# First keys and their tail in one tile, tails of four heads stacked, small loads as rows, and another order of the opening transfers

## The chip, the cores and the metric

One core of a Trainium2 chip. The metric is the device time of one execution in microseconds, as a median of several runs; smaller is better.

## The reference

Eight batches, each of eight heads, 576 tokens and 64 columns per head. 32 pack rows per head attend to keys and values; the tokens' queries then attend to the packed rows; the result, 512 wide, goes through one of eight experts.

```python
p_packed = sm_attn(p, k, v)               # (8, 8, 32, 64): 32 rows per head
out = sm_attn(q, p_packed, p_packed)      # (8, 8, 576, 64)
x = out.transpose(0, 2, 1, 3).reshape(8, 576, 512)
logits = x @ w_gate                       # 8 experts
local_gate = sigmoid(x @ w_local)
...
e = argmax(logits[b, s]) if s == 0 or local_gate[b, s] < 0.5 else prev_e
p = softmax(logits[b, s])
out[b, s] = p[e] * (relu(x[b, s] @ w1[e]) @ w2[e])
```

The kernel computes every token of a batch with the expert of the batch's first token, and computes a batch again where a count of other tokens says so; with these inputs that count is nought.

## The kernel before, in words

All of a batch's attention is small beside the two layers of its expert. The first layer (`layer1`, L939) multiplies the attention weights by the product of packed values and w1, split in a high and a low part (wph, wpl; `pack_quarters`, L870 to L882 in the first batch); the second layer (`layer2`, L967 to L976) multiplies by w2, split likewise (`splits`, L925 and L927). Heads are handled in two sets Q of four.

For the first batch, nothing can be hidden behind another batch, and the expert must be known before its weights can be loaded. So the opening is a chain: packs and keys are loaded (`loads`, `load_packs`, `load_tokens`) and turned in place on VectorE (`turn_keys`, L377); scores of a Q are 32-row products on TensorE, with the 64 tail tokens of a head as products of their own (`scores`, L443 and L453); VectorE takes their minima (L463, L474), ScalarE the exponential (L488), TensorE turns the weights (`keys`, L497 and L501), multiplies by the values (L521) and turns the packed values (L541). `early_choice` computes the first token's expert from q0, its eight query columns (L682 to L714); `gate_weights` (L655) needs wgl, which holds w_gate and w_local. The expert's number goes to SyncE (`choose`, L672), which then issues the weights (`weights`, L823 and L836, in the order of `FIRST`). Meanwhile the queries of the first batch, and the keys and queries of the second, are turned by TensorE transposes and ScalarE copies, head by head (`turn_tokens`, L391, L392, L394), and `queries` (L571) and `soften` (L591 to L635) make the attention weights of the tokens, in two parts.

Each of these is a generator. A planner (`weave`) steps them in an order that it works out while the program is built: `Clock` holds a due time for each engine and tile, from prices in the code (`price`, L98 to L125; a DMA by its bytes over `clock.rate`, plus 2000 ns while it starts before 25 us, L137 to L153). The result is a fixed order of instructions per engine, and each engine runs its own in order. Where TensorE would be without work by that clock, `keep_warm` adds fillers, products of ones that nobody reads (L214, two passes each), one for each 240 ns of the gap (`FILL`, L1149), until the third piece of the first layer. Work of a batch later than the one that still lacks its expert is stepped only when the engines named in `by` are free in the planner's clock (the factor 0.0 in L1139); before, the second batch's turns need only their data.

DMAs are issued in order by SyncE (nc.sync) or ScalarE (nc.scalar), the issuing engine waiting for a free buffer first. Buffers are counted by tag in `BUFS`: five of "kv", two of "w1t", eight of "w2s", five of "o", two of "p_in". The first batch's keys and values take four of the five "kv" buffers and its queries start on the fifth.

## Time and profile before

| | us |
|---|---|
| median of 3 runs | 431.51 (431.38 to 431.62) |
| the profiled execution | 431.04 |
| its span | 429.0 |
| TensorE matmuls busy | 413.5 (96%) |
| VectorE busy | 295.4 (69%) |
| ScalarE busy | 178.8 (42%) |

The span runs from the first to the last instruction that the profile shows; some 2 us of the time lie around it. Busy time of TensorE counts fillers too, and the ends of matmuls are modelled, so 96% doesn't mean that it works at its peak. Where a line of the profile gives a count for TensorE, it counts passes: a product of 32-bit floats takes two, a transpose of 128 rows one. Times below are from the start of the span.

### The profile page before, as it was taken

Reading aid. Unit: us, or ns where it says so; the run is one execution under the profiler, and the core shown is the slowest. Engines: PE = TensorE matmul, PEld = TensorE weight load, DVE = VectorE, ACT = ScalarE, POOL = GpSimd, SP = SyncE. Lnnn points to the kernel's source line nnn. Section 1 sums busy time; section 2 is a strip of 40 time slices with the busy share of each in tenths; the row PEclk is TensorE's granted clock in tenths of the full one; section 3 lists DMA queues with packets and bytes.
Section 4 is the critical chain, followed back from the end, with each engine's and each line's share of the span. In section 5 each row is a group of like instructions: output and inputs, shape, how many; then the busy total and the mean of one; then the engine's idle time right before and its main releaser. Section 6 shows DMA issues by size and latency. Waiting matters only on the chain.

```text
span 429.0 us, 10275 instructions
## 1 busy us (share of the span) xinstructions
PE 413.5 (96%) x3958; PEld 329.0 (77%) x3959; DVE 295.4 (69%) x859; ACT 178.8 (42%) x419; POOL 36.3 (8%) x56
## 2 busy tenths in 40 slices
PE   8799999999999999998999999999999999999994
PEld 8666688867887688777887688777887688878883
DVE  4368679798974797838877697838877697546221
ACT  1356734265333544254443643345433544244221
POOL 2000620300110002000030002000020002000000
PEclk9999999999999999999999999999999999999999
DMA  8889799367998289976999199964999340634011
GB/s 226 183 257 317 229 135 154 84 243 229 141 162 295 73 220 131 152 273 200 168 146 317 63 242 136 187 242 149 197 122 273 113 147 0 235 122 147 0 63 56
DMA packets 167271, 73.24 MB, mean 171 GB/s; under 512 B 129072, under 2 KB 147248, under 8 KB 167216
## 3 DMA queue, kind: packets, MB, share of 16 engines
q1 hardware_dynamic: 166528, 72.13, 75.5%
q8 instruction: 33, 0.54, 0.6%
q10 hardware_dynamic: 688, 0.39, 0.3%
q14 instruction: 22, 0.18, 0.2%
HBM read 63.07 MB, written 9.44 MB: 169 GB/s over the span
## 4 chain that ended last, share of the span: by engine, by line
PE 73%; DMA 9%; DVE 8%; SPq 6%; issue 2%; ACT 1%; POOLq 0%; DVEq 0%; POOL 0%; ACTq 0%
PE bank L967 33%; PE bank L939 19%; DMA qn<-in_q_dram 6%; SPq L307 4%; PE bank L972 3%; PE bank L976 3%; DVE wpl L913 2%; PE bank L571 2%; PE bank L521 2%; PE bank L899 2%; PE bank L443 2%; DVE qn L555 1%; PE bank L497 1%; DMA kv<-in_q_dram 1%; PE bank L391 1%
## 5 line engine op out<-in xcount | busy, mean ns | idle before, releaser
L967 PE MATMUL bank<-w2s,h 128*128 128x512 f32 x768 | 207.3, 400 | 3.9 <-DVE w2s L927 3.2
L967 PEld LDWEIGHTS bank<-w2s,h 128*128 128x128 f32 x768 | 135.4, 188 | 35.6 <-DVE w2s L927 4.9
L954 DVE SCALAR_TENSOR_TENSOR h<-bank,h 128x256 fp32r<-128x256 f32 x192 | 61.3, 347 | 60.0 <-ACT h L950 59.4
L950 ACT ACTIVATE h<-bank 128x256 fp32r<-128x256 f32 (+1 forms) x128 | 52.7, 412 | 118.7 <-PE bank L939 111.1
L939 PEld LDWEIGHTS bank<-a2h,wph 128*128 128x128 f32 x256 | 47.0, 188 | 16.2 <-ACT wph L910 1.3
L939 PE MATMUL bank<-a2h,wpl 128*128 128x320 f32 (+1 forms) x256 | 56.3, 298 | 0.4 <-DVE wpl L913 0.2
L939 PE MATMUL bank<-a2h,wph 128*128 128x320 f32 (+1 forms) x256 | 56.4, 301 | 0.2
L939 PE MATMUL bank<-a2l,wph 128*128 128x320 f32 (+1 forms) x256 | 54.9, 296 | 0.0
L635 POOL TENSOR_TENSOR a2l<-a2t,a2h 128x576 fp32r<-128x576 f32 (+2 forms) x17 | 23.0, 1355 | 294.6 <-ACT a2h L632 294.6
L939 PEld LDWEIGHTS bank<-a2h,wpl 128*128 128x128 f32 x256 | 41.3, 188 | 1.8 <-DVE wpl L913 1.6
L939 PEld LDWEIGHTS bank<-a2l,wph 128*128 128x128 f32 x256 | 40.9, 188 | 0.0
L925 ACT CAST w2s<-w2raw 128x512 fp32r<-128x512 f32 x64 | 37.4, 622 | 2.8 <-DMA w2raw<-in_moe_w_dram 2.8
L927 DVE TENSOR_TENSOR w2s<-w2raw,w2s 128x512 fp32r<-128x512 f32 x58 | 37.4, 680 | 1.3 <-ACT w2s L925 1.3
L972 PE MATMUL bank<-w2s,h 128*128 128x512 f32 x64 | 25.3, 396 | 0.0
L976 PE MATMUL bank<-w2s,h 128*64 128x512 f32 x64 | 25.0, 391 | 0.0
L591 DVE STREAM_TRANSPOSE sT<-bank 128x288 f32<-128x288 f32 (+2 forms) x36 | 13.2, 420 | 10.4 <-ACT gate L589 8.4
L913 DVE TENSOR_TENSOR wpl<-bank,wph 128x512 fp32r<-128x512 f32 x28 | 18.0, 680 | 2.4 <-ACT wph L910 2.4
L910 ACT CAST wph<-bank 128x512 fp32r<-128x512 f32 x28 | 14.9, 595 | 10.8 <-PE bank L899 10.8
L488 ACT ACTIVATE a<-a,nb 128x576 f32<-128x576 f32 x16 | 12.4, 776 | 16.3 <-DVE nb L474 16.3
L463 DVE TENSOR_SCALAR_CACHE_REDUCE a<-bank 128x288 f32<-128x288 f32 (+2 forms) x36 | 13.6, 421 | 6.0 <-PE bank L453 3.8
L632 ACT CAST a2h<-a2t 128x576 fp32r<-128x576 f32 (+2 forms) x18 | 11.2, 622 | 13.8 <-DVE a2t L626 9.5
L214 PE MATMUL bank<-warm 128*128 128x128 f32 x88 | 15.8, 335 | 1.1 <-DVE warm L209 1.1
(139 smaller groups left out, 454.0 us busy)
## 6 DMA issues: line engine op xcount, KB each, us to landing
w2raw<-in_moe_w_dram SPq DMA_DIRECT2D x64, 256.0 KB, 6.3
w1t<-in_moe_w_dram SPq DMA_DIRECT2D x14, 1024.0 KB, 6.7
kv<-in_v_dram SPq DMA_DIRECT2D x16, 512.0 KB, 6.5
out_dram<-o SPq DMA_DIRECT2D x31, 256.0 KB, 2.3
qn<-in_k_dram SPq DMA_DIRECT2D x24, 288.0 KB, 7.1
qn<-in_q_dram SPq DMA_DIRECT2D x24, 288.0 KB, 6.9
kv<-in_q_dram SPq DMA_DIRECT2D x8, 256.0 KB, 4.5
w1t<-in_moe_w_dram SPq DMA_DIRECT2D x4, 512.0 KB, 7.3
```

The source lines that it names most:

```text
L214: nc.tensor.matmul(out=warm_ps[:, :128], lhsT=warm, rhs=warm, start=True, stop=True)
L307: nc.sync.dma_start(out=x[ps_].rearrange("i h (c j) -> i (h c) j", j=32), in_=rows[r, a])
L635: eng.tensor_tensor(out=a2l, in0=a2t, in1=a2h.bitcast(F32), op=ALU.subtract)
L913: nc.vector.tensor_tensor(out=lo[fh][:, Q], in0=ts[fh, Q], in1=hi[fh][:, Q].bitcast(F32), op=ALU.subtract)
L925: nc.scalar.copy(out=w[:, 0], in_=raw)
L927: (nc.gpsimd if st["early"] and c > 1 else nc.vector).tensor_tensor(out=w[:, 1], in0=raw, in1=w[:, 0].bitcast(F32), op=ALU.subtract)
L939: nc.tensor.matmul(out=t[:, :GROUP * (m1 - m0)], lhsT=st["wp"][c // 4][wi][:, Q, fs], rhs=a2[ai][Q][:, GROUP * m0:GROUP * m1], start=(n == ...
L950: nc.scalar.activation(out=h[:, :w], in_=t[:, :w], func=AF.Relu)
L954: nc.vector.scalar_tensor_tensor(out=h[:, dst:dst + z - a], in0=t[:, a:z], scalar=0.0, in1=h[:, a:z].bitcast(F32), op0=ALU.max, op1=ALU.su ...
L967: nc.tensor.matmul(out=acc, lhsT=hs[hi], rhs=w[:, wi], start=(c == 0 and n == 0), stop=(c == NC - 1 and n == 2),)
L972: nc.tensor.matmul(out=acc, lhsT=h[:, 256:WIDE + TAIL], rhs=w[:, 0], start=(c == 0), stop=False, skip_group_check=True,)
L976: nc.tensor.matmul(out=acc[0:TAIL], lhsT=h[:, 256:WIDE], rhs=w[:, 1], start=False, stop=(c == NC - 1), skip_group_check=True,)
```

## The change

- The first batch's keys and their tail lie in one tile "kf" on the tag "w1t" (later the first weights' buffers), 5 x 64 columns per head. Q0's keys come in two transfers of two heads on SyncE and its tail on ScalarE's queue; all four pack transfers are on ScalarE's queue. A turn of the packs is a step of its own, ahead of the keys'.
- A score product takes the tail's 32 columns along: 160 columns where r is 0 or 1, 128 else. The products of the tail (L453) are gone.
- The 64 tail tokens of four heads are loaded as one 128 x 128 tile (tag "w2s", before "o"), and turned by one transpose and one copy. The other 512 tokens come in one transfer with four tokens per partition; they are turned two heads at a time, four transposes and one copy of 512 columns.
- q0 and w_local are loaded as sixteen rows of 64 (tile "small") on ScalarE's queue, after Q0's keys, turned by TensorE and copied to their places by VectorE; w_gate follows on the same queue.
- The second batch's packs are loaded after its keys and queries, not ahead of them. The first batch's query turns wait for both Q's value products, the second batch's turns for both first parts of the first batch's `queries`.
- In `keys` of the first batch the tail's transpose shares the bank that ScalarE reads.

```diff
...
+    small = const.tile([2 * H, D], F32, name="small")
...
+    def load_keys(Q):
+
+        x = tile_([128, HQ, (NJ + 1) * D], F32, "kf", "w1t")
+        rows = k[0].rearrange("(h q) s d -> q h s d", q=NQ)[Q]
+        clock.rate = 300.0
+        for hs in (slice(0, HQ // 2), slice(HQ // 2, HQ)) if Q == 0 else (slice(0, HQ),):
+            nc.sync.dma_start(out=x[:, hs, 0:NJ * D], in_=rows[hs, 0:512].rearrange("h (p c) d -> p h (c d)", c=NJ))
+        clock.rate = 200.0
+        (nc.scalar if Q == 0 else nc.sync).dma_start(out=x[0:TAIL, :, NJ * D:], in_=rows[:, 512:S].rearrange("h p d -> p h d"))
+        return x
+
+    def load_small():
+
+        clock.rate = 100.0
+        nc.scalar.dma_start(out=small[0:H], in_=q[0, :, 0, :])
+        nc.scalar.dma_start(out=small[H:2 * H], in_=w_local.rearrange("(h d) e -> h (d e)", d=D))
+        with nc.allow_non_contiguous_dma(reason="rows of 8 elements"):
+            nc.scalar.dma_start(out=wgl[:, :, 0:E], in_=w_gate.rearrange("(h d) e -> d h e", d=D))
+
+    def turn_small():
+
+        yield need(small, banks=1, when=lambda: sts[0]["scored"] > 0)
+        tp = bank()
+        nc.tensor.transpose(out=tp[0:D, 0:2 * H], in_=small, identity=ident[0:2 * H, 0:2 * H])
+        yield need(tp, by=("DVE",))
+        nc.vector.tensor_copy(out=q0[:, :, 0:1], in_=tp[0:D, 0:H].unsqueeze(2))
+        nc.vector.tensor_copy(out=wgl[:, :, E:E + 1], in_=tp[0:D, H:2 * H].unsqueeze(2))
+        give(tp)
+        sts[0]["small"] = True
...
     def load_pairs(src, b, Q):
 
-        x = tile_([128, HQ, 2, 2 * D], F32, "kv")
-        rest = tile_([TAIL // 2, HQ, 2 * D], F32, "qt", "o")
+        x = tile_([128, HQ, NJ * D], F32, "kv")
+        rest = tile_([128, 2 * D], F32, "qt", "w2s")
         rows = at(src, b).rearrange("(h q) s d -> q h s d", q=NQ)[Q]
-        clock.rate = 320.0
-        for c in range(2):
-            nc.sync.dma_start(out=x[:, :, c], in_=rows[:, 256 * c:256 * c + 256].rearrange("h (p r) d -> p h (r d)", r=2))
+        clock.rate = 300.0
+        nc.sync.dma_start(out=x, in_=rows[:, 0:512].rearrange("h (p c) d -> p h (c d)", c=NJ))
         clock.rate = 200.0
-        nc.sync.dma_start(out=rest, in_=rows[:, 512:S].rearrange("h (p r) d -> p h (r d)", r=2))
+        nc.sync.dma_start(out=rest, in_=rows[:, 512:S].rearrange("h (p r) d -> h p (r d)", r=2))
         return x, rest
...
-            st["p"] = load_packs(b, (nc.sync, nc.scalar, nc.sync, nc.scalar))
+            st["p"] = load_packs(b, (nc.scalar,) * 4)
...
-            order = (("p", 1), ("k", 0), ("k", 1), ("q", 0), ("q", 1)) if st["second"] else \
+            order = (("k", 0), ("k", 1), ("q", 0), ("q", 1), ("p", 1)) if st["second"] else \
...
+            yield need(slot="p_in" if name == "p" else "qn" if blocks else "kv" if name == "v" else "w1t" if st["early"] and name == "k" else ("kv", "w2s"))
...
-                st[name, Q] = load_tokens(x, b, Q) if name == "k" and st["early"] else load_pairs(x, b, Q)
-            if st["early"] and (name, Q) == ("v", 1):
-                clock.rate = 100.0
-                with nc.allow_non_contiguous_dma(reason="512 elements"):
-                    nc.sync.dma_start(out=q0[:, :, 0:1], in_=q[0, :, 0:1, :].rearrange("h s d -> d h s"))
-                    nc.sync.dma_start(out=wgl[:, :, 0:E], in_=w_gate.rearrange("(h d) e -> d h e", d=D))
-                    nc.sync.dma_start(out=wgl[:, :, E:E + 1], in_=w_local.rearrange("(h d) e -> d h e", d=D))
+                st[name, Q] = load_keys(Q) if name == "k" and st["early"] else load_pairs(x, b, Q)
+            if st["early"] and (name, Q) == ("k", 0):
+                load_small()
...
-        yield need(slot="qn", when=lambda: (name, 0) in st and (st["second"] or "a2t" in st))
+        yield need(slot="qn", when=lambda: (name, 0) in st and ("a2t" in st if st["early"] else sts[0]["asked"] >= NQ))
...
-            yield need(when=lambda: (name, Q) in st)
+            yield need(when=lambda: (name, Q) in st and (st["second"] or st["valued"] == NQ and (Q == 0 or st["ppT"][Q] is not None)))
             x, rest = st[name, Q]
-            for h in range(HQ):
-                yield need(x, rest, banks=1, by=("Activation",))
+            for hs in (slice(0, 2), slice(2, 4)):
+                yield need(x, banks=1, by=("Activation",))
                 tp = bank()
-                for c in range(2):
-                    nc.tensor.transpose(out=tp[:, 128 * c:128 * c + 128], in_=x[:, h, c], identity=ident)
-                nc.tensor.transpose(out=tp[:, 256:HALF], in_=rest[:, h], identity=ident[:TAIL // 2, :TAIL // 2])
+                for n in range(4):
+                    nc.tensor.transpose(out=tp[:, 128 * n:128 * n + 128], in_=x[:, hs][:, n // 2, 128 * (n % 2):128 * (n % 2) + 128], identity=ident)
                 yield need(tp, by=("Activation",))
-                nc.scalar.copy(out=xT[:, Q, h], in_=tp[:, :HALF])
+                nc.scalar.copy(
+                    out=xT[:, Q, hs, 0:256].rearrange("a h (p c) -> a h c p", c=2), in_=tp.rearrange("a (h c p) -> a h c p", h=2, c=2),
+                )
                 give(tp)
+            yield need(rest, banks=1, by=("Activation",))
+            tp = bank()
+            nc.tensor.transpose(out=tp[:, 0:128], in_=rest, identity=ident)
+            yield need(tp, by=("Activation",))
+            nc.scalar.copy(out=xT[:, Q, :, 256:HALF], in_=tp[:, 0:128].rearrange("a (h x) -> a h x", h=HQ))
+            give(tp)
...
-            yield need(when=lambda: ("k", Q) in st and "p" in st)
-            yield need(*st["k", Q])
-            for x in st["k", Q]:
-                turn(x)
-
-            st["kT", Q] = st["k", Q][0].rearrange("a h (c x i) -> a h x c i", c=NJ, x=2)
-        if Q == 0:
+            yield need(when=lambda: ("k", Q) in st and "pT" in st)
+            x = st["k", Q]
+            yield need(x)
+            for y in (x[:, 0:2, 0:NJ * D], x[:, 2:4, 0:NJ * D]) if Q == 0 else (x[:, :, 0:NJ * D],):
+                nc.vector.transpose(out=y, in_=y)
+            y = x[0:TAIL, :, NJ * D:]
+            nc.vector.transpose(out=y, in_=y)
+
+            st["kT", Q] = x.rearrange("a h (c x i) -> a h x c i", c=NJ + 1, x=2)
...
+    def turn_packs(st):
+
+        yield need(when=lambda: "p" in st)
+        yield need(st["p"])
+        turn(st["p"])
+        st["pT"] = st["p"].rearrange("a h (x n) -> a h x n", n=NP)
...
+                    cs = NJ + (r < 2)
                     for h in range(HQ):
                         nc.tensor.matmul(
-                            out=ts[Q, r][32 * h:32 * h + 32, :512 // n if n == 4 else HALF],
+                            out=ts[Q, r][32 * h:32 * h + 32, :32 * cs if n == 4 else HALF],
                             lhsT=st["pT"][ps_, NQ * h + Q, x],
-                            rhs=st["kT", Q][ps_, h, x] if st["early"] else st["kT", Q][ps_, h],
-                            start=(x == 0), stop=(x == steps - 1),
-                        )
-            for x in range(steps if st["early"] else 0):
-                for r in range(2):
-                    ps_ = slice(rows * r, rows * r + rows)
-                    for h in range(HQ):
-                        nc.tensor.matmul(
-                            out=ts[Q, r][32 * h:32 * h + 32, 128:160],
-                            lhsT=st["pT"][ps_, NQ * h + Q, x],
-                            rhs=st["k", Q][1][ps_, h, NP * x:NP * x + NP],
+                            rhs=st["kT", Q][ps_, h, x, 0:cs] if st["early"] else st["kT", Q][ps_, h],
                             start=(x == 0), stop=(x == steps - 1),
                         )
...
-            nc.tensor.transpose(out=tps[1][:TAIL, 256:384], in_=sc[:, 512:S], identity=ident)
+            rest = tps[0 if st["early"] else 1][:TAIL, 256:384]
+            nc.tensor.transpose(out=rest, in_=sc[:, 512:S], identity=ident)
             if st["early"]:
...
-            nc.scalar.copy(out=a_rest[Q][:TAIL], in_=tps[1][:TAIL, 256:384])
+            nc.scalar.copy(out=a_rest[Q][:TAIL], in_=rest)
...
+        st["valued"] += len(Qs)
...
-        if part != 0:
-            st["asked"] += len(Qs)
-        if st["asked"] == NQ:
+        st["asked"] += len(Qs)
+        if st["asked"] == NQ * (1 + st["early"]):
...
+        yield need(when=lambda: None not in st["ppT"] and "small" in st)
+        yield need(*st["ppT"], wgl, banks=1)
...
+            yield need(when=lambda: st["ppT"][Q] is not None and "small" in st)
...
+                    *((turn_packs(st), early_choice(st), turn_small()) if early else ()),
...
```

## Rows read from the trace of the kernel before

**Rows 1.** Busy time by stretch, core 0: from:to in us, length, then TensorE (PE), weight loads (PEld), VectorE (DVE), ScalarE (ACT) and GpSimd (POOL) busy with their instructions, granted clock, DMA share, GB/s; and the line of the fillers from the groups of instructions from 0 to 45 us (busy us, mean ns | idle before).

```profile
0.00:38.20 38.20, 33.74 (x548) 26.47 (x549) 20.52 (x77) 14.53 (x41) 3.31 (x18) 1.00 0.86 236
...
45.00:424.00 379.00, 372.94 (x3349) 298.15 (x3335) 269.76 (x766) 159.44 (x367) 31.73 (x37) 1.00 0.76 163
...
L214 PE MATMUL bank<-warm 128*128 128x128 f32 x88 | 15.8, 335 | 1.1 <-DVE warm L209 1.1
```

**Rows 2.** The chain that ended last, from 26.9 to 45 us, in order of time: start us, us, what.

```profile
28.06 0.37 PE bank L391 x2
28.43 0.17 PE bank L392
...
33.37 0.59 PE bank L870 x16
33.96 1.09 PE bank L214 x8
...
36.78 0.38 PE bank L571 x16
...
38.25 1.08 PE bank L939 x6
...
42.48 0.64 PE bank L214 x4
```

**Rows 3.** Timeline of TensorE's matmuls from 0 to 45 us: start us, us, engine, line, operation, out<-in, passes [idle before, releaser].

```profile
1.10 8.09 PE L214 MATMUL bank<-warm 128*128 128x128 f32 x44 [1.10 <-DVE warm L209]
9.12 0.96 PE L443 MATMUL bank<-kv,p_in 32*32 32x128 f32 x57
...
9.98 0.47 PE L453 MATMUL bank<-kt,p_in 32*32 32x32 f32 x29
...
14.72 0.32 PE L453 MATMUL bank<-kt,p_in 32*32 32x32 f32 x22 [2.11 <-issue]
...
20.18 1.03 PE L521 MATMUL bank<-kv,a1T 128*32 128x64 f32 x32
...
26.12 0.31 PE L704 MATMUL bank<-gate,et 128*32 128x32 f32 x4
...
28.53 0.51 PE L571 MATMUL bank<-qn,ppT 64*32 64x160 f32 x16
```

**Rows 4.** The DMA view of short windows. First a queue's line in 11.50 to 11.75 us (packets, MB, share of 16 engines), then issues (out<-in, queue, operation, count, KB each, median us from issue to landing): packs of the first batch issued on ScalarE's queue in 1.2 to 1.7 us, the first keys' tail in 2.2 to 2.9, w_local in 9.2 to 10.3, packs of the second batch in 15.85 to 17.8, the first weights in 28.5 to 29.

```profile
q8 instruction: 1, 0.02, 40.5%
...
p_in<-in_p_dram ACTq DMA_DIRECT2D x2, 64.0 KB, 2.8
...
kt<-in_k_dram SPq DMA_DIRECT2D x1, 64.0 KB, 4.4
...
wgl<-in_moe_w_local_dram SPq DMA_DIRECT2D x1, 2.0 KB, 5.1
...
p_in<-in_p_dram SPq DMA_DIRECT2D x4, 32.0 KB, 5.2
...
w1t<-in_moe_w_dram SPq DMA_DIRECT2D x1, 512.0 KB, 3.8
```

**Rows 5.** Timeline of VectorE from 0 to 45 us, columns as in group 3.

```profile
8.00 0.66 DVE L377 STREAM_TRANSPOSE p_in<-p_in 128x512 f32<-128x512 f32 x1
8.59 1.20 DVE L377 STREAM_TRANSPOSE kv<-kv 128x1024 f32<-128x1024 f32 x1
9.72 0.39 DVE L377 STREAM_TRANSPOSE kt<-kt 64x256 f32<-64x256 f32 x1
...
11.49 0.16 DVE L474 TENSOR_REDUCE nb<-m 128x1 f32<-128x4 f32 x1
...
22.84 0.25 DVE L690 STREAM_TRANSPOSE es<-bank 128x64 f32<-128x64 f32 x1 [1.08 <-PE bank L682]
...
24.84 0.24 DVE L701 STREAM_TRANSPOSE et<-es 128x64 f32<-128x64 f32 x1
...
27.37 0.14 DVE L669 TENSOR_SCALAR e<-ecd 1x1 int32<-1x1 f32 x1
...
35.75 0.75 DVE L882 TENSOR_TENSOR wpl<-bank,wph 128x256 fp32r<-128x256 f32 x2
```

**Rows 6.** ScalarE: two lines of its timeline from 0 to 40 us (columns as in group 3), its line of copies from the groups of 0 to 45 us, and the page's group of 512-column casts (busy us, mean ns | idle before, releaser).

```profile
1.76 1.28 ACT L488 ACT_TABLE_LOAD   x1 [1.63 <-PEq L1256]
11.68 0.78 ACT L488 ACTIVATE a<-a,nb 128x576 f32<-128x576 f32 x1 [8.64 <-DVE nb L474]
...
L394 ACT COPY qn<-bank 128x288 f32<-128x288 f32 x24 | 9.4, 400 | 4.9 <-PE bank L392 4.1
...
L910 ACT CAST wph<-bank 128x512 fp32r<-128x512 f32 x28 | 14.9, 595 | 10.8 <-PE bank L899 10.8
```

**Rows 7.** Timeline of the DMAs that SyncE's queue issues, from 0 to 60 us: start us, us that the issue took, line, out<-in, count.

```profile
1.73 0.45 SPq L277 DMA_DIRECT2D kv<-in_k_dram  x1
...
7.75 1.46 SPq L368 DMA_DIRECT2D wgl<-in_moe_w_gate_dram  x1
...
10.47 3.22 SPq L289 DMA_DIRECT2D kv<-in_q_dram  x2
...
14.35 0.92 SPq L289 DMA_DIRECT2D kv<-in_q_dram  x2
...
28.54 0.40 SPq L836 DMA_DIRECT2D w1t<-in_moe_w_dram  x1
```

15 lines of the change are left out of this document (5 added, 10 removed).

## The prediction

> **What bounds the kernel now.** I read the busy times by stretch first [rows 1]. Between 45 and 424 us TensorE is busy 372.9 of 379 us, so nothing can be won there but by less TensorE work, and the change leaves that stretch alone. Up to the first product of the network's first layer, at 38.2 us, it is idle for 4.5 us, and a good part of its busy time is filler: 88 passes of L214, 15.8 us in all. The reader is to see that the time is the moment at which the first layer starts, plus the TensorE work still undone then, plus a tail that stays.
>
> Then the chain of waits [rows 2]: from 28 us on it holds TensorE alone, and in its order turns, fillers and packing of weights alternate until L939 at 38.25. There the length of TensorE's own queue sets the time, fillers included. Then TensorE's timeline ahead of that [rows 3]: 44 filler passes, scores of Q0 at 9.12, scores of Q1 broken off for 2.11 us by nothing that the profile names, the values' products of Q1 at 20.18, the early choice's product at 26.12. The DMA view shows what the break may be [rows 4]: the core's one instruction packet of that time starts between 11.5 and 11.75 us, when the queue is full of 4-byte elements (w_local's 2 KB take 5.1 us to land). Then VectorE [rows 5], ScalarE [rows 6] and SyncE's issues [rows 7]: the choice's last step ends at 27.51, the first weights are issued at 28.54.
>
> **The change part by part**, on the clock of the profiled run (span 429.0 us, its time 431.04, so 2.04 us outside; the median 431.51 is 0.47 above it). The planner decides the order and the number of fillers; I work its due times by hand from the code. They give order and counts, no times. Durations are the rows'.
>
> *First transfers.* Key and pack transfers start together: the first half of the keys is the first issue of SyncE, not the third at 1.73 [rows 7]; ScalarE issues four pack pieces at some 0.45 each by 2.6, the last landing at 2.6 + 2.8 = 5.4 at worst, the tail, fifth on that queue, by 3.4 + 4.4 = 7.8 [rows 4]. VectorE, done with packs and keys by 7 (0.66 and 1.20 [rows 5]), needs 0.39 for the tail. Ready about 7.5 to 8.3, against 8.66 before. It gains nothing: the planner waits for all of tile kf, whose last transfer, the tail, is due at 6524 ns; 160 later TensorE, at 5400 after the first 10 fillers, gets (6684 - 5400)/240 = 5; three turns make the scores due at 8626, and (8626 - 6542)/240 = 8 more: 23, where the same working for the kernel before gives 10 + 4 + 8 = 22, and 22 of two passes are the 44 of the row [rows 3]. Two more passes at 1.09/8 = 0.136 [rows 2]: the scores of Q0 start at 9.4, 0.25 later. That hides 1.1 to 1.9 us of late landing; without the cover such lateness would count in full.
>
> *Scores of 160 columns.* 64 passes for 96: 57 passes took 0.96 with 0.27 of latency in it, 12 ns each, and half are a quarter longer: 0.85 for 1.26 from 9.12 to 10.45. VectorE's minima and nb need 1.2 after (10.45 to 11.65): nb at 11.45. Exp 0.78 [rows 6], at 12.3. The planner has 9 fillers here (18 passes, 2.45 us), so L497 at 12.8.
>
> *Keys of Q1.* In the planner's order their turn now comes behind Q0's minima (it stood ahead at 8.59 [rows 5]): 1.20 + 0.39 from 11.45, scores of Q1 at 13.35 to 14.2, nb at 15.35. The break of 2.11 us: before, it came after 44 + 96 + 8 + 74 passes, with a weight load each; now as many are run through only some 24 passes into the values' products, at 14.4, and the packet that it may wait for is asked for no later. Cost between 0 and 2.1; I take 0, since the only such packet's long wait fell on 1,024 four-byte elements that are now sixteen rows.
>
> *Values, second Q.* Exp 15.4 to 16.2, L497 at 16.5, products at 17.8 (before 20.18), the packed values' transpose at 19.4, since a unit of query turns stands ahead of it. The a_rest copy without its wait on VectorE saves 0.2, included.
>
> *The choice.* Gate products by 20.5; VectorE's chain took 22.84 to 25.08, 2.24, to which I add 0.1 for a ScalarE copy ahead of its exp: 22.85. L704 comes 1.1 after that chain before; now no second batch's turn can stand there (it needs "asked" of both Q), only a query unit and one filler: 23.2. e0 ended 1.4 after L704's start (26.12 to 27.51), with transposes of VectorE in between; without them 1.0: 24.2, 3.3 earlier. SyncE: its last issues ahead (q of Q1 and four pack pieces, 0.45 each) wait for a kv buffer read at about 20.2 and end at 23.3, so they are no block. Weights issued at 25.25, landed at 29.05 [rows 4].
>
> *Turns of four heads.* Before, a head is 0.37 + 0.17 = 0.54, a unit of four 2.16 [rows 2]. After, nine 128-wide transposes of 0.185: 1.67. Six units: 2.9 us less TensorE work. ScalarE: 4 copies of 0.400 become two of about 0.6 (the 512-column copy's 0.595) and one of 0.26: 1.46 for 1.60 [rows 6]. So L571 of Q1 at 23.45 to 23.9 (before 28.53).
>
> *From there to the first layer.* VectorE's way from that L571 to the end of wpl took 28.53 to 36.5, 8.0; it would allow 31.4, and 1.5 more if VectorE has to wait for the second batch's packs, now loaded last (issued by 23.3, landing up to 5.2 later, 28.5 [rows 4], with its softmax queued behind): 31.4 to 32.9. TensorE's queue is longer: of the second batch's four units I count 2.1 in the planner's gap (22.7 to 30.3 on its clock, 7.6, less 2.0 for other ScalarE work, at 2.7 each), 3.5 us; L870 0.59, two L571 0.76, and 18 fillers of two passes (7.6 less 3.3 planned work, by 0.24), 4.9: 23.9 + 9.75 = 33.7 for 38.2, 4.5 earlier. Undone are 1.9 units, 3.2 us, where before three heads (1.62) and 0.64 of filler were: 0.9 given back. Net 3.6.
>
> *The other way round:* TensorE work less 2.9 + 0.8; idle 4.5 to 1.4, 3.1 less; fillers 118 passes for 88, 4.0 more: 2.8. I take the middle of 2.8 and 3.6, near 3.3: 428.2 on the median. Its own range 426.0 to 430.2: 1.1 less if no filler costs more than its cover, 2.1 more for the break.
>
> A page of the Trainium skill, "Runtime: NRT & Kernel Launch", section "Instruction fetch mechanics", speaks against the gain from the break: instruction blocks are fetched ahead and crossing one is mostly hidden. By that rule the 2.11 us would have another cause and stay; the trace, with one packet and one break side by side, speaks against it, but it shows that only once.
>
> **The rivals.** *More:* the units of the second batch fit before the first layer entirely, in place of fillers. 33.0 for L939 and nothing left: 38.2 - 33.0 + 1.62 + 0.64 = 7.4, so 424.1. For it: TensorE has 9 us there, the work is 6.7 + 1.4; against: the planner starts a unit of a later batch only when ScalarE is free in its own clock. *The break stays* wherever it now falls, on the chain since Q1's way sets all that follows: 3.3 - 2.1 = 1.2, so 430.3. For it: the data queue is as full as before. *Slower:* ScalarE, in order, is held by its own eight transfers. The same small loads on SyncE were followed by two query issues that took 3.22 instead of 0.92 [rows 7], because the queue took no more. If w_gate's issue holds ScalarE until w_local's landing before, 14.4, its table load of 1.28 [rows 6] and exp follow at 15.7 for 11.5: 4.2 less 3.3, 0.9 slower, 432.4. It decides from an exp later than 14.9; at 10 or less it costs nothing. Against: that queue now holds 0.34 MB, not 2.5. *The change does nothing:* should every unit of the second batch fall behind the first layer (6.7 us undone, 5.1 more, less 0.6 of filler), 4.5 is given back in full: 431.5.
>
> **How the numbers follow.** Chances: forecast 0.54, more 0.16, the break stays 0.13, nothing 0.08, slower 0.09. What a measurement can tell from no change is about 0.2%, 0.9 us: faster is under 430.65. The break case lies at that border and I give it 0.10 faster, 0.03 same. Faster 0.80, same 0.11, slower 0.09. The range 424.0 to 431.6 leaves out the slower case, and the half of the first rival below its value.
>
> **What would show it.** Right: 46 filler passes ahead of scores at 9.3 to 9.5; no break of more than 0.5 us before 20; first weights issued at 24.5 to 26; L939 at 33 to 34.5 with about two units of L391 after it; TensorE's busy time from 45 on unchanged in its steps. Wrong: exp of Q0 after 13; L939 later than 36; a wait of VectorE on p_in of over 1 us amid its softmax; new idle time of TensorE between L939 and 60 us on w2s or w1t.

## The result, and the profile after

The changed kernel takes 435.92 us (435.73 to 436.10), the kernel before on the same chip 431.56 (431.38 to 431.83): a ratio of 1.01, 95% interval 1.0083 to 1.0118, 4.4 us slower, where 428.2 was forecast with 424.0 to 431.6 as its range. Its profiled execution has a span of 434.0 us, the forecast's was 425.7 (428.2 less 2.04 around the span and the 0.47 between median and profiled run). In the changed file L443 is L486 (scores), L488 L521 (exp), L497 L530, L521 L555 (values' products), L704 L738, L836 L870 (issue of the first matrix's quarters, w1t), L870 L904 (their product), L939 L973 (first layer), L967 L1001 (second layer); a unit of turns is L416 twice and L424 once. Some executions of a kernel run at a lower granted clock throughout; the ratios leave them out, and the profiled one of e15 below is of that kind.

TensorE's timeline of the changed kernel from 0 to 50 us, in the columns of [rows 3]:

```profile
1.10 6.75 PE L214 MATMUL bank<-warm 128*128 128x128 f32 x46 [1.10 <-DVE warm L209]
13.32 1.63 PE L486 MATMUL bank<-kf,p_in 32*32 32x160 f32 x64 [5.47 <-DVE kf L449]
...
15.04 3.71 PE L214 MATMUL bank<-warm 128*128 128x128 f32 x20
...
29.08 0.31 PE L738 MATMUL bank<-gate,et 128*32 128x32 f32 x4
...
38.19 0.56 PE L973 MATMUL bank<-a2h,wph 128*128 128x320 f32 x2
...
40.86 2.40 PE L214 MATMUL bank<-warm 128*128 128x128 f32 x20
...
46.38 0.67 PE L904 MATMUL bank<-w1t,ppT 64*32 64x256 f32 x16 [0.84 <-DMA w1t<-in_moe_w_dram]
```

The 46 filler passes are there as predicted, but they end at 7.85, and TensorE then waits 5.47 us for the tail of the keys. The scores of Q0 start at 13.32 (9.12 before [rows 3], 9.4 forecast). All the same the first layer starts at 38.19, where it did before (38.18). The choice's product is at 29.08 (26.12 before, 23.2 forecast). So the whole loss against the kernel before stands behind that point: from it to the end are 395.8 us, before 390.8, and 392.0 in the forecast. The forecast is missed twice, by 4.5 us ahead of the first layer and by 3.8 behind it.

VectorE's timeline of the same run, its two waits for the first transfers:

```profile
10.44 0.71 DVE L402 STREAM_TRANSPOSE p_in<-p_in 128x512 f32<-128x512 f32 x1 [8.76 <-DMA p_in<-in_p_dram]
...
12.83 0.44 DVE L449 STREAM_TRANSPOSE kf<-kf 64x256 f32<-64x256 f32 x1 [0.49 <-DMA kf<-in_k_dram]
```

ScalarE's timeline, the transfers that it issues (ACTq: start, duration of the issue) and its first work:

```profile
0.78 4.39 ACTq L344 DMA_DIRECT2D p_in<-in_p_dram  x4
5.73 0.76 ACTq L280 DMA_DIRECT2D kf<-in_k_dram  x1
...
10.14 0.66 ACTq L289 DMA_DIRECT2D wgl<-in_moe_w_gate_dram  x1
10.82 1.28 ACT L521 ACT_TABLE_LOAD   x1 [10.70 <-DMA p_in<-in_p_dram]
16.13 0.78 ACT L521 ACTIVATE a<-a,nb 128x576 f32<-128x576 f32 x1 [4.02 <-DVE nb L507]
```

The four packs took 4.39 us to issue, not 1.8, and were there at 10.44; the tail, fifth on that queue, at 12.83. The DMA view of 4 to 8 us says whose packets were served (q1 is SyncE's queue, q10 ScalarE's: packets, MB, share of 16 engines; then issues of that stretch with us from issue to landing):

```profile
q1 hardware_dynamic: 1252, 1.04, 98.6%
q10 hardware_dynamic: 495, 0.12, 14.0%
...
p_in<-in_p_dram ACTq DMA_DIRECT2D x1, 64.0 KB, 5.6
kf<-in_k_dram ACTq DMA_DIRECT2D x1, 64.0 KB, 7.1
```

Both queues are fed, q10 gets 2 packets of some 250 bytes to 5 of some 830, a tenth of the bytes. Last, busy time by stretches of 1 us (columns as in [rows 1]; the third number from the end is TensorE's granted clock):

```profile
9.00:10.00 1.00, 0.00 (x0) 0.00 (x0) 0.00 (x0) 0.00 (x0) 0.00 (x0) 1.00 1.12 210
10.00:11.00 1.00, 0.00 (x0) 0.00 (x0) 0.56 (x1) 0.17 (x1) 0.00 (x0) 0.89 1.13 324
11.00:12.00 1.00, 0.00 (x0) 0.00 (x0) 1.00 (x3) 1.00 (x1) 0.00 (x0) 0.50 0.68 122
...
17.00:18.00 1.00, 1.00 (x8) 1.00 (x8) 0.69 (x4) 0.00 (x0) 0.00 (x0) 0.70 0.71 216
```

TensorE, idle from 7.85 on, was granted 0.50 (1.2 of 2.4 GHz) from 11 to 17 us; the 20 filler passes behind the first scores then took 3.71 us (18 in 2.45 were forecast), the scores themselves 1.63 (1.12 at the full clock, as in e4 below).

### The profile page after: what moved, and what is told of

Read it like the earlier page. It is cut to its first block, busy times and chain, and to the rows that moved or that the text cites. A ratio compares the mean times of both kernels' runs of the same rounds, so it can differ in the third digit from the quotient of the medians.

```text
span 434.0 us, 10237 instructions
## 1 busy us (share of the span) xinstructions
PE 414.8 (96%) x3939; PEld 332.5 (77%) x3940; DVE 295.0 (68%) x862; ACT 178.0 (41%) x413; POOL 36.6 (8%) x56
## 4 chain that ended last, share of the span: by engine, by line
PE 77%; DVE 8%; DMA 8%; issue 2%; ACT 2%; SPq 1%; POOLq 0%; POOL 0%; DVEq 0%; ACTq 0%
PE bank L1001 35%; PE bank L973 20%; PE bank L1006 3%; PE bank L1010 3%; DMA qn<-in_q_dram 3%; DMA kf<-in_k_dram 3%; PE bank L486 2%; PE bank L555 2%; DVE wpl L947 2%; PE bank L214 2%; PE bank L933 2%; DMA w1t<-in_moe_w_dram 2%; PE bank L606 2%; PE bank L530 2%; DVE qn L590 1%
## 5 line engine op out<-in xcount | busy, mean ns | idle before, releaser
L1001 PE MATMUL bank<-w2s,h 128*128 128x512 f32 x768 | 207.9, 400 | 4.5 <-DVE w2s L961 3.1
L1001 PEld LDWEIGHTS bank<-w2s,h 128*128 128x128 f32 x768 | 135.3, 188 | 36.1 <-issue 5.3
L973 PEld LDWEIGHTS bank<-a2h,wph 128*128 128x128 f32 x256 | 47.1, 188 | 16.7 <-issue 1.7
L973 PE MATMUL bank<-a2h,wph 128*128 128x320 f32 (+1 forms) x256 | 56.8, 302 | 0.1
L973 PE MATMUL bank<-a2h,wpl 128*128 128x320 f32 (+1 forms) x256 | 56.3, 298 | 0.4 <-DVE wpl L947 0.2
L973 PE MATMUL bank<-a2l,wph 128*128 128x320 f32 (+1 forms) x256 | 54.6, 294 | 0.0
L973 PEld LDWEIGHTS bank<-a2h,wpl 128*128 128x128 f32 x256 | 41.0, 188 | 1.8 <-DVE wpl L947 1.6
L973 PEld LDWEIGHTS bank<-a2l,wph 128*128 128x128 f32 x256 | 41.1, 188 | 0.0
L214 PE MATMUL bank<-warm 128*128 128x128 f32 x150 | 21.9, 303 | 1.1 <-DVE warm L209 1.1
L214 PEld LDWEIGHTS bank<-warm 128*128 128x128 f32 x150 | 20.5, 216 | 1.6 <-DVE warm L209 0.8
L944 ACT CAST wph<-bank 128x512 fp32r<-128x512 f32 x28 | 14.9, 596 | 10.8 <-PE bank L933 10.8
L521 ACT ACTIVATE a<-a,nb 128x576 f32<-128x576 f32 x16 | 12.4, 776 | 13.3 <-DVE nb L507 13.3
L666 ACT CAST a2h<-a2t 128x576 fp32r<-128x576 f32 (+2 forms) x18 | 11.2, 621 | 14.2 <-DVE a2t L660 9.3
```

The source lines that it names most:

```text
L214: nc.tensor.matmul(out=warm_ps[:, :128], lhsT=warm, rhs=warm, start=True, stop=True)
L944: nc.scalar.copy(out=hi[fh][:, Q], in_=ts[fh, Q])
L973: nc.tensor.matmul(out=t[:, :GROUP * (m1 - m0)], lhsT=st["wp"][c // 4][wi][:, Q, fs], rhs=a2[ai][Q][:, GROUP * m0:GROUP * m1], start=(n == ...
L1001: nc.tensor.matmul(out=acc, lhsT=hs[hi], rhs=w[:, wi], start=(c == 0 and n == 0), stop=(c == NC - 1 and n == 2),)
```

## Theories, and the experiments

*Queue:* packs and tail are late because ScalarE's queue is served badly beside a full SyncE queue; with that undone the forecast comes true. *Rival 1, second batch:* its packs, loaded last, and its turns, held back, are what costs. *Rival 2, small loads:* the sixteen rows and the gate's weights on ScalarE cost. When the first runs had come, a further theory was needed for what is lost behind the first layer. Times are medians; the kernel before on the same chips was at 431.6 to 432.2, with more scatter than above.

The stages of all runs, from TensorE's and SyncE's timelines of the profiled executions, in us (break: idle time of TensorE by "issue" within the opening; rest: from the first layer's start to the span's end):

```
                          scores  break  weights  first   rest   span
                          of Q0          issued   layer
before                      9.12   2.11   28.54   38.18   390.8  429.0
forecast                    9.4    0      25.25   33.7    392.0  425.7
after                      13.32   none   31.28   38.19   395.8  434.0
e1_packs_split              8.59   0.66   25.92   33.90   394.7  428.6
e2_tail_sync               10.65   none   29.03   35.56   399.2  434.8
e3_both                     8.71   2.03   29.08   35.72   396.9  432.6
e4_fillers                 14.07   none   30.27   37.47   396.1  433.6
e5_packs_first              7.77   1.48   25.75   34.00   394.8  428.8
e6_turns_free               9.02   0.66   27.19   34.78   398.0  432.8
e7_weights_first            9.20   1.20   27.34   33.95   399.5  433.4
e9_quarters_then_values     8.47   1.03   26.35   33.03   401.3  434.3
e10_quarters_and_turns      7.94   1.30   26.60   34.19   395.7  429.9
e11_and_early_splits        9.28   2.03   30.12   37.70   393.4  431.1
e12_all_and_filled          9.08   1.76   30.23   37.23   394.5  431.7
e13_wide_fillers            8.18   none   27.60   35.18   392.5  427.7
e14_packs_and_wide          8.54   none   25.48   33.48   394.7  428.2
```

Each row is one execution. It lies within 0.6 us of its kernel's median in before, after, e1, e5, e7, e10 and e13, but 1.1 above it in e4, 1.8 to 3.3 above it in e2, e3, e6, e9, e11 and e12, and 1.1 below it in e14. What a change is worth is therefore read from the medians and ratios, and the rows say where time goes in that one execution.

### e1_packs_split: the packs alternate between SyncE and ScalarE again

```diff
-            st["p"] = load_packs(b, (nc.scalar,) * 4)
+            st["p"] = load_packs(b, (nc.sync, nc.scalar, nc.sync, nc.scalar))
```

> The kernel after, with the first batch's four pack transfers alternating between SyncE and ScalarE as before; the first keys' tail stays on ScalarE's queue, now third there. Theory (queue): behind a full SyncE queue the packets of ScalarE's queue come late, packs at 10.4 and tail at 12.8 us; here the packs land by about 5 and the tail by 9, the first scores start at 9.5 to 10.5 and the time is 429 to 432. Rival 1 (second batch): the loss comes from the second batch's turns and packs, put later; this changes nothing there, so the scores start earlier but the time stays at 434 to 436. Rival 2 (small loads): they hold ScalarE's queue; the time stays near 435.

Measured: 430.60 beside 431.96, ratio 0.998 (0.9948 to 1.0011). VectorE's timeline of this run:

```profile
4.07 0.71 DVE L402 STREAM_TRANSPOSE p_in<-p_in 128x512 f32<-128x512 f32 x1 [2.49 <-DMA small<-in_moe_w_local_dram]
...
6.84 0.39 DVE L449 STREAM_TRANSPOSE kf<-kf 64x256 f32<-64x256 f32 x1
```

and TensorE's:

```profile
14.99 0.38 PE L555 MATMUL bank<-kv,a1T 128*32 128x64 f32 x11 [0.66 <-issue]
...
30.97 0.67 PE L904 MATMUL bank<-w1t,ppT 64*32 64x256 f32 x16 [1.05 <-DMA w1t<-in_moe_w_dram]
...
33.90 0.56 PE L973 MATMUL bank<-a2h,wph 128*128 128x320 f32 x2
...
36.55 2.39 PE L214 MATMUL bank<-warm 128*128 128x128 f32 x20
...
45.45 0.71 PE L486 MATMUL bank<-qn,p_in 64*32 64x288 f32 x16
```

With two of the four packs on the other queue they are turned at 4.07, not 10.44, the tail, still on ScalarE, at 6.84, and the first layer starts at 33.90, forecast 33.7. (The releaser in brackets is inferred and names another load; in e3 the same wait, 2.52 us to 4.11, is put down to p_in.) The small loads stood where the change put them: rival 2 falls. Rival 1, by which the time had to stay at 434 to 436, falls as the whole cause. But only 1.4 us of the forecast's 3.3 are there, and the interval holds none as well. Behind the first layer 20 filler passes stand, and the second batch's scores come at 45.45 (43.05 before).

### e2_tail_sync and e3_both: the tail on SyncE, alone and together with e1's edit

```diff
-        (nc.scalar if Q == 0 else nc.sync).dma_start(out=x[0:TAIL, :, NJ * D:], in_=rows[:, 512:S].rearrange("h p d -> p h d"))
+        nc.sync.dma_start(out=x[0:TAIL, :, NJ * D:], in_=rows[:, 512:S].rearrange("h p d -> p h d"))
```

> The kernel after, with the first keys' tail on SyncE's queue behind the keys; all four pack transfers stay on ScalarE's queue. Theory (queue): the packs still land at 9 to 10.4 us and VectorE turns them first, then 1.26 of keys and 0.44 of tail, so the scores start at 11.8 to 13 and the time is 433.5 to 435.5; the packs are the larger part. Were the tail alone the cause: scores at 9.5, 430. Rival 1 (second batch) and rival 2 (small loads): 435 to 436.

> The kernel after, with both on their queues as before: packs alternating, the tail on SyncE; only the three small loads are left on ScalarE's queue. Theory (queue): scores at 9.4 right behind the fillers, first weights issued at 25 to 26, first layer at 33.5 to 34.5, time 427.5 to 429.5, the prediction's value for the whole change. Rival 1 (second batch): 434 to 436 in spite of early scores. Rival 2 (small loads): they alone hold up the packs on that queue, scores later than 11, 433 or more.

Measured: e2 433.23, ratio 1.0016 (0.9987 to 1.0044); e3 431.76, ratio 0.9992 (0.9961 to 1.0023). VectorE in e2:

```profile
8.38 0.71 DVE L402 STREAM_TRANSPOSE p_in<-p_in 128x512 f32<-128x512 f32 x1 [6.70 <-DMA p_in<-in_p_dram]
```

TensorE in e3:

```profile
16.48 0.53 PE L555 MATMUL bank<-kv,a1T 128*32 128x64 f32 x10 [2.03 <-issue]
...
17.26 2.47 PE L214 MATMUL bank<-warm 128*128 128x128 f32 x10
...
45.13 0.67 PE L904 MATMUL bank<-w1t,ppT 64*32 64x256 f32 x16 [2.08 <-DMA w1t<-in_moe_w_dram]
```

Without the tail behind them the packs on ScalarE's queue are 2 us earlier than in the changed kernel, and earlier than the 9 to 10.4 expected, but still 4.3 later than in e1. In e2 the clock falls too: TensorE idles 2.25 us ahead of the scores, is granted 0.50 from 12 to 15 us, and the 20 filler passes take 4.13 us. e3, for which 427.5 to 429.5 was expected, missed. It opens as well as e1 and, in the profiled execution, loses it to something else: after 20 passes of the values' products TensorE stops for 2.03 us, the ten filler passes behind run at the lower clock (0.50 from 17 to 19 us; 2.47 us for 1.38 in e1), and the weights are issued 3.2 us later. The rival *The break stays* came true here, at the place that the prediction had worked out for it.

### e4_fillers: the changed kernel with 23 fillers more at the start

```diff
-    keep_warm(WARM)
+    keep_warm(WARM + 23)
```

> The kernel after, with 23 more fillers ahead of the first scores, unknown to the planner, so that TensorE is busy to about 13.1 us and does not idle for 5.5 us; no transfer is moved. Theory (queue, with the granted clock's fall as its second half): the clock stays up, the first scores take 0.85 for 1.63 and the 20 fillers behind them 2.4 for 3.7, and about 2.0 us comes off the time: 433.5 to 434.5; the rest of the loss stays. If the clock doesn't matter: 435.5 to 436.

Measured: 434.25, ratio 1.0042 (1.0007 to 1.0076). TensorE in e4, and its stretch from 9 to 19 us (clock third from the end; 0.66 in the same stretch of the changed kernel):

```profile
14.07 1.12 PE L486 MATMUL bank<-kf,p_in 32*32 32x160 f32 x64
...
15.25 2.50 PE L214 MATMUL bank<-warm 128*128 128x128 f32 x20
...
9.00:19.00 10.00, 10.00 (x195) 9.28 (x199) 5.62 (x20) 2.68 (x5) 0.00 (x0) 1.00 0.85 231
```

The packs are just as late (turned at 11.18), the scores start 0.75 later than after, but the granted clock is 1.00 from 9 to 19, the scores take 1.12 and the filler passes behind them 2.50, and the weights are issued 1.0 earlier. So the fallen clock, by itself, is worth 1.1 us by the spans (0.4 less, from scores 0.75 later) and 1.8 by the weights' issue; the ratios differ by 2.5 us, uncertain by 1.7. e1, which ends the waiting as well, takes back 5.2 us by the ratios: the waiting is the larger part.

### e8_before_packs_act: the kernel before with its packs on ScalarE

```diff
-            st["p"] = load_packs(b, (nc.sync, nc.scalar, nc.sync, nc.scalar))
+            st["p"] = load_packs(b, (nc.scalar,) * 4)
```

> The kernel before with one edit: its four first pack loads all issued by ScalarE, as in the changed kernel. Theory (pieces of 256 bytes in ScalarE's queue are served behind the full SyncE queue, whatever else is changed): packs ready after 8 instead of at 8.0 by some 1.5 to 4 us, scores at 10 to 12.5 instead of 9.12, TensorE idle and its clock down, 2 to 5 us slower than the kernel before. Rival (the loss needs the changed kernel's other loads, tail and small loads on ScalarE): packs turned by 8.5, scores by 9.6, within 0.6 us of the kernel before.

Measured: 431.92 beside 431.59, ratio 1.0024 (0.999 to 1.0058). VectorE, then TensorE in this run:

```profile
8.11 0.71 DVE L377 STREAM_TRANSPOSE p_in<-p_in 128x512 f32<-128x512 f32 x1 [1.39 <-DMA p_in<-in_p_dram]
...
8.88 0.96 PE L443 MATMUL bank<-kv,p_in 32*32 32x128 f32 x57 [0.33 <-DVE p_in L377]
```

The theory missed here: it expected scores at 10 to 12.5 and 2 to 5 us lost. The rival came true: packs turned by 8.5, scores by 9.6, the same time. The packs do land later. They take 4.2 us from issue to landing in the median, where two on that queue took 2.8 [rows 4], though ScalarE issued all four in 2.02 us, and VectorE, done with its first keys, waits 1.39 us for them. It costs nothing, because the fillers keep TensorE busy until 8.55 and it waits 0.33 us after that. So the packs' place alone does not make the loss; the changed kernel's other loads, the tail behind the packs or what SyncE issues at that time, belong to it.

### e5_packs_first and e6_turns_free: the second batch's packs first again; its turns not held

```diff
-            order = (("k", 0), ("k", 1), ("q", 0), ("q", 1), ("p", 1)) if st["second"] else \
+            order = (("p", 1), ("k", 0), ("k", 1), ("q", 0), ("q", 1)) if st["second"] else \
```

```diff
-        yield need(slot="qn", when=lambda: (name, 0) in st and ("a2t" in st if st["early"] else sts[0]["asked"] >= NQ))
+        yield need(slot="qn", when=lambda: (name, 0) in st and (st["second"] or "a2t" in st))
```

> The kernel of e1_packs_split with the second batch's packs loaded ahead of its keys and queries again. In e1 they were issued at 21.97 and turned at 40.97, and the second batch's scores began at 45.45 (43.05 in the kernel before), with 20 filler products (2.39 us) between the first layer and the second. Theory (after the first layer TensorE lacks work that is ready, and what the early choice gained is given back there): scores of the second batch come back to 41 to 43, they take the fillers' place in part, 0.5 to 1.5 us faster than e1, so 429.1 to 430.1 beside a kernel before of 431.9. Rival (only what is left undone counts, in any order): the packs' 128 KB push keys and queries back by 0.4 us, the same time as e1 within 0.4.

> The kernel of e1_packs_split with the second batch's turns no longer held until the choice's vectors stand. In e1 the first of them was at 26.54 and 2.0 units of four were undone when the first layer began at 33.90. Theory (what is undone at the first layer is paid after it): turns take the place of fillers before 26.5 where keys have landed, the undone part falls to 1 to 1.5 units, 0.8 to 1.7 us faster than e1, unless they delay the choice. Rival (the turns compete with the choice on TensorE and ScalarE): the weights are issued 0.5 us or more later than 25.92, and the time is that of e1 or up to 1 us slower.

Measured: e5 430.49, ratio 0.9982 (0.9952 to 1.0012); e6 431.47, ratio 1.0001 (0.9975 to 1.0027). Each is made on e1. e5 is e1's time and has its 20 filler passes, and scores at 45.76: the rival's forecast, and no effect of the packs' place is seen. e6 takes the filler passes down to 2 and 8, with scores at 37.74, and gains nothing; here too it is the rival that came true, with the weights issued at 27.19, 1.3 later than in e1 (0.4 of it already at the first scores). Its TensorE:

```profile
43.82 1.38 PE L904 MATMUL bank<-w1t,ppT 64*32 64x256 f32 x16 [2.94 <-DMA w1t<-in_moe_w_dram]
```

What took the fillers' place is done before the third quarter of the first matrix arrives. But that quarter is issued at 34.74 in e6 and at 32.40 in e1, so most of this wait goes with a later issue; that e1's fillers had covered a wait for weights is not shown.

### e7_weights_first and e9_quarters_then_values: the third and fourth quarter ahead of the second batch's values

```diff
-FIRST = "1 2 1 2 2 v 1 2 1 2 2 2 2".split()
+FIRST = "1 2 1 2 2 1 2 1 2 v 2 2 2".split()
```

(e7, on e1; in e9 the string is "1 2 1 2 2 1 2 1 v 2 2 2 2": 1 is a quarter of the first matrix, 2 a piece of the second, v the second batch's values.)

> The kernel of e1_packs_split with the four quarters of the expert's first matrix and their second-matrix rows ahead of the second batch's values on SyncE. In e1 the second batch's values (1.15 MB) stood between the second and the third quarter; the third was issued at 32.40 and its product came at 41.16, behind 20 fillers. Theory (the first layer's second half waits for its weights and the fillers cover that wait): the third quarter is issued at 29 to 30, its product comes at 37 to 38, and the time is 1 to 2 us below e1. Rival (DMA is full from 25 us on, so an earlier quarter only makes other loads late, and the second layer waits for w2 instead): within 0.5 us of e1.

> The kernel of e1_packs_split with the second batch's values placed behind the fourth quarter of the expert's first matrix and the first four pieces of its second, so ahead of the pieces that wait for a buffer. In e7_weights_first the values stood behind a piece that waited for a buffer until 38.30; they were issued at 38.68 instead of 29.71, and the third batch's packs at 56.51 instead of 47.55; TensorE then waited 2.99 us for the third batch at 91.53 and its granted clock was 0.83 from 90 to 100. Theory (the loss of e7 is this chain of late loads, not the order of the quarters): values at 32 to 34, third batch's packs at 47 to 50, no wait at 85 to 95, third quarter's product at 38 to 39, and the time is 0.5 to 2 us below e1 (428.6 to 430.1). Rival (the values themselves are what the second batch lacks): as slow as e7, 434 to 435.

Measured: e7 434.92, ratio 1.0079 (1.0054 to 1.0103); e9 433.79, ratio 1.0063 (1.0032 to 1.0095). In e7 neither forecast came: 1 to 2 us less than e1, or the same within 0.5, was expected, and it is some 4 us more. e7 starts the first layer when e1 does, e9 0.9 us earlier; both lose far behind it. TensorE in e9:

```profile
38.02 0.67 PE L904 MATMUL bank<-w1t,ppT 64*32 64x256 f32 x16 [1.95 <-DMA w1t<-in_moe_w_dram]
...
92.71 0.75 PE L530 MATMUL bank<-ident,a 128*128 128x128 f32 x4 [2.99 <-ACT a L521]
```

and its stretch from 90 to 100 us (clock third from the end):

```profile
90.00:100.00 10.00, 7.29 (x55) 4.42 (x56) 7.44 (x23) 5.87 (x13) 0.00 (x0) 0.83 0.52 188
```

My theory of e9, that the values issued in time (31.36 instead of 38.68) would keep the third batch in time, fell: the second of the third batch's values is again issued only at 56.09 and its packs at 58.25 (47.55 in e1), and the wait of 2.99 us is there. The order that the planner then writes has nothing between the third batch's scores and the transposes that wait for its exp; in e1 six passes of the second layer, 1.66 us, stand there. The rival's time, 434 to 435, nearly came; its reason was not tested.

### e10, e11, e12: quarters and turns; early splits; the gap at the third batch filled

On e1, e10 has e6's edit and e9's string. e11 adds

```diff
-            yield need(when=lambda: len(st.get("w2", ())) > c and (not st["early"] or "begun" in st))
+            yield need(when=lambda: len(st.get("w2", ())) > c and (not st["early"] or st["wq"] > 0))
```

and e12 has the string "1 2 1 2 2 1 v 2 1 2 2 2 2" in its place.

> The kernel of e9_quarters_then_values with the second batch's turns no longer held until the choice's vectors stand, as in e6_turns_free. In e6 the second batch was turned when the first layer began, its scores came at 37.74 instead of 45.45, fillers after the first layer were 2 and 8 instead of 20, but the product of the third quarter waited 2.94 us for its weights at 43.82 and the granted clock fell to 0.91 over 38 to 58. Theory (both are needed, what is ready and the weights' third quarter): no wait over 0.5 us at 36 to 46, the first layer at 34.0 to 34.8, 1.5 to 3 us below e1, 427.6 to 429.1. Rival (the choice delayed by turns ahead of it takes all that is won): 430 to 431.5.

> The kernel of e10_quarters_and_turns with the splits of the expert's second matrix allowed from the first quarter of weights on, not from the first layer's start. In e1 the first split's copy ran on ScalarE at 36.54 and its difference ended on VectorE at 38.2, which is what the second layer began on at 38.70. Theory (the second layer waits for the splits, with fillers as cover): first split's copy at 32 to 34, six fillers fewer between the layers, 0.3 to 0.8 us below e10. Rival (ScalarE and VectorE are behind with the weights' casts there, so an earlier split makes those later and the first layer begins later by as much): equal to e10 or up to 0.7 us slower.

> The kernel of e11_and_early_splits with one place changed: the second batch's values stand behind the third quarter of the expert's first matrix, not behind the fourth. The written order then has the second layer's products of the batch before between the third batch's scores and the transposes that wait for its exp; in e11 nothing stood there and TensorE waited 2.02 us at 90.04. In e11 the first layer began at 37.70, because the break in the values' products took 2.03 us and the granted clock fell behind it (0.93 over 0 to 24), and yet at 68.5 it was only 0.7 us behind e1, whose first layer began at 33.90. Theory (what the early choice wins is given back by fillers, a late third quarter and late splits, and by what is next behind them): no wait over 1 us at 85 to 95, and 427.5 to 430 where the kernel before is at 432.0; with a break under 1.5 us the first layer at 34 to 35. Rival (each place that is mended opens another, and what is won before the first layer cannot be kept): within 0.5 us of e1, 430 to 431.5.

Measured: e10 431.87, ratio 1.0015 (0.9975 to 1.0055); e11 431.07, 0.9984 (0.9966 to 1.0002); e12 430.18, 0.9962 (0.9942 to 0.9982). e10 misses its 427.6 to 429.1 and lies just above its rival's 430 to 431.5: with a first layer at 34.19 its rest is 395.7. What the early splits are worth isn't shown. e11's first split is copied on ScalarE 1.2 us ahead of the first layer (0.15 behind its start in e10, 2.6 in e1), and the rest falls to 393.4 in spite of a wait of 2.02 us at 90.04; but the first layer itself starts 3.5 us later there, which alone may shorten the rest, and the two ratios differ by 0.3% with more than that as their uncertainty. In e12 no wait over 0.6 stands from 85 to 100, as intended. Its 430.18 lies between the two forecasts, 427.5 to 430 and the rival's 430 to 431.5, and is the first to be clearly faster than the kernel before, by 0.8 to 2.5 us. Both profiled runs of e11 and e12 begin the first layer 3 us later than e10: 1.3 and 1.1 of it stand already at the first scores, the rest comes by the break and the clock behind it, as in e3 (the ten filler passes took 1.38 in e10). TensorE in e11:

```profile
17.05 0.38 PE L555 MATMUL bank<-kv,a1T 128*32 128x64 f32 x11 [2.03 <-issue]
...
17.60 2.50 PE L214 MATMUL bank<-warm 128*128 128x128 f32 x10
...
37.70 0.54 PE L973 MATMUL bank<-a2h,wph 128*128 128x320 f32 x2
```

### e13, e14, e15: the same filler time in fewer instructions

```diff
-        for _ in range(n):
+        for _ in range(n // 4):
+            nc.tensor.matmul(out=warm_ps[:, :512], lhsT=warm, rhs=warm.unsqueeze(1).to_broadcast([128, 4, 128]), start=True, stop=True)
+            clock.until["PE"] = clock.engine("PE") + 45.0
+        for _ in range(n % 4):
             nc.tensor.matmul(out=warm_ps[:, :128], lhsT=warm, rhs=warm, start=True, stop=True)
```

(The added line on the planner's clock keeps the order of work the same.) e13 is e12 with it, e14 e1, e15 the kernel before.

> The kernel of e12_all_and_filled with every four fillers in a row written as one product of 512 columns: the same filler time in fewer instructions, 18 products (36 passes) fewer ahead of the values' products. Theory (the break stands behind a count of instructions, and the next block arrives at 15 to 17 us): the break leaves the values' products and moves about 36 passes on, to the first query's transposes at 17 to 18, where it costs 0 to 0.6; no fall of the granted clock over 9 to 24; 0.7 to 1.7 us below e12, so 428.5 to 429.5 where the kernel before is at 431.9. Rival (the break is tied to a time or to a load that is late there, not to the count): 0.66 to 2.03 us at 14 to 17 as before, within 0.5 us of e12.

> The kernel of e1_packs_split with the same wide fillers. Theory (count of instructions): no break in the values' products, 0.5 to 1.5 us below e1, 429.0 to 430.1 where the kernel before is at 431.9. Rival (time or load): break of 0.66 to 2.03 at 14 to 17, within 0.5 us of e1.

> The kernel before with the same wide fillers: 12 products (24 passes) fewer ahead of the break, which moves past the rest of the second scores' tail (22 passes) to the fillers behind it. Theory (count of instructions): the second scores end at 12.7 instead of 15.04, the break stands before the transposes of the first query's exp and is partly covered by the wait for it; 0.5 to 1.8 us faster than the kernel before. Rival (time or load): the break stays in the second scores' tail at 12.6, same time within 0.5 us.

Measured: e13 429.00 beside 431.91, ratio 0.9929 (0.9903 to 0.9955); e14 431.07, 0.9984 (0.9964 to 1.0003); e15 430.87, 0.9974 (0.9943 to 1.0006). e13 is the fastest of all, 2.9 us below the kernel before. Its TensorE:

```profile
13.36 0.65 PE L558 MATMUL bank<-kv,a1T 128*32 128x64 f32 x32
13.83 0.29 PE L558 MATMUL bank<-v_rest,a_rest 128*32 128x64 f32 x8
14.05 1.12 PE L214 MATMUL bank<-warm 128*128 128x512 f32 x2
...
35.18 0.54 PE L976 MATMUL bank<-a2h,wph 128*128 128x320 f32 x2
```

No "issue" stands in its opening any more: the 40 passes run through, and the clock is 1.00 from 9 to 19. 36 passes on, where the count puts the break, TensorE comes at about 16, and no idle time is left there. (Its largest wait up to the first layer is now one of 2.19 us at 19.92, for the keys of the second batch.) In e15 the break moved too, from the second scores' tail to the fillers behind it:

```profile
14.45 0.94 PE L217 MATMUL bank<-warm 128*128 128x128 f32 x6 [1.91 <-issue]
```

Nothing else is read from e15's profiled execution, 438.1 us; its median is 1.1 us below the kernel before, and the interval holds none as well as the 0.5 to 1.8 expected. The count of instructions sets the place: the break stands behind 220 passes in all nine kernels that have it with the small loads as rows, and behind 222 in the kernel before, e8 and e15, in e15 with other products among them. e13 and e14 show only that it is gone. What that gains is another matter. e13 and e12 differ by 1.4 us in the ratios, uncertain by as much. e14's weights are issued 0.4 us earlier than e1's and its first layer starts 0.4 earlier, which is about what e1's break of 0.66 left to win in that execution; the first quarter's product still waits for its weights:

```profile
30.56 0.67 PE L907 MATMUL bank<-w1t,ppT 64*32 64x256 f32 x16 [1.65 <-DMA w1t<-in_moe_w_dram]
```

The time is e1's, where 0.5 to 1.5 less was expected.

## Why the prediction was wrong, step by step

- **First transfers**: this step failed, and first. It took the packs' landing as 2.8 us, from ScalarE's queue when it held two packs, and the tail's as 4.4, from a transfer on SyncE's queue [rows 4], and issue times of 0.45. With all four packs there the issue took 4.39, the last pack 5.6 to land and the tail 7.1: ready at 13.3 against 7.5 to 8.3. The cover of 1.1 to 1.9 us was rightly put, but the lateness went far beyond it, and a clock at half for six microseconds, of which no step spoke, came on top. By the ratios e1 takes back 5.2 us of the changed kernel's time, e2 3.6 and both together (e3) 4.7: either move alone takes back most, so the two loads are not two separate losses, and the clock that e4 prices is within e1's share. Why the tail behind them makes the packs themselves 2 us later (8.38 in e2, 10.44 after) stays open: what is on SyncE's queue changes with it.
- **Scores, keys and values of Q1, the choice**: right in order once the opening is mended, and the end point near by some luck. e1 issues the weights at 25.92 (25.25) and starts the first layer at 33.90 (33.7). But its scores start 0.8 earlier than forecast, and from them to the weights it takes 17.3 for 15.9, 0.66 of the difference being the break.
- **The break**: the prediction moved it to "some 24 passes into the values' products" and priced it 0 to 2.1, taking 0, since the four-byte elements were gone. The place was right (20 passes), the value taken was wrong: 0.66 to 2.03 in nine experiments with the small loads as rows. It is none in after, e2 and e4, whose TensorE comes to the values' products at 17.5 or later. The break stays without those elements, so they are not what it needs.
- **From there to the first layer** and behind it: the second failed step. "0.9 given back" was counted from undone turns alone, with no filler left behind the first layer; 5.0 us more than before lie there. In the windows from there to the end TensorE is busy 383.3 us (379.8 before) and idle 12.6 (11.1). The turns are as forecast: two units are undone where 1.9 were counted. The term put at nothing is the filler: 20 passes, 2.40 us, where the kernel before has 4. With it and the wait of 0.84 for the third quarter, the 0.9 become 4.1 of the 5.0; the rest is open. The sum *the other way round* counted fillers too, but only up to the first layer. The prediction's own sign, new idle time on w1t before 60 us, stands in the timeline of after. What each place behind the first layer is worth (fillers, third quarter, splits, third batch) isn't separated by e6, e7 and e9 to e12; e13, with all of them changed, has a rest of 392.5, near the forecast's 392.0.
- **The sum's own range**: its lower end doesn't follow from its terms, since 428.2 less 1.1 is 427.1, not 426.0; nothing hangs on it.
- **The rivals.** *Slower* gave 432.4 and exp from 14.9 on as the point that decides; exp came at 16.13. Yet its mechanism isn't what delayed it: ScalarE was held by its own transfers until 10.80 and had its table by 12.1, and then waited 4.02 us for VectorE's nb. Its premise against it, that this queue holds only 0.34 MB, proved no protection. *The break stays* (430.3) is nearest to e3, 431.8. *More* and *nothing* did not occur.

The Trainium skill's rule that the prediction weighed, from "Runtime: NRT & Kernel Launch", section "Instruction fetch mechanics", that crossing a block of instructions is mostly hidden, doesn't hold in this opening, if the break is such a crossing: it is paid in twelve of the seventeen profiled kernels, with 0.66 to 2.11 us, and hidden in those that come late to it or, as e13 and e14, have fewer instructions ahead of it. Where the prediction used its row against that rule, the row was the better guide, though the sum then didn't follow the row.

## What to carry to other kernels

Price a transfer that is moved to another queue by how that queue fares beside what else is running, not by a landing time from an idle one, and ask first what its lateness would hold up: the same move of the packs cost nothing in the kernel before and, beside the changed kernel's other loads, stopped that one. A gain ahead of a stage must be followed through the next two waits (weights, splits, the next batch) before it is counted, and fillers that remain there are a term of the sum. When an engine stops at the same instruction in every run and nothing is named, fewer instructions ahead of it are a cheap test, and here part of the best version, 429.0 us against 431.9.
